# Sparse attention and a Fourier-mix block on one core: weight conversion on VectorE in a fixed plan, and two constant matmuls at each score step of the first attention

## The chip, the cores and the metric

The kernel runs on one core of one Trainium2 chip. The metric is the device time of one execution in microseconds. The engines are PE (TensorE, matmuls; PEld its weight loads), DVE (VectorE), ACT (ScalarE), POOL (GpSimd) and SP (SyncE, which issues nearly all DMAs). Each engine runs its own instructions in order.

## The reference

Four batches of 768 tokens; attention with 8 heads of 64, then a channel block of width 512 to 2048 and back. All in float32, but the two weights arrive as float64.

```python
k_sum = k.reshape(B, H, nb, block, D).max(axis=3)       # nb = 24 blocks of 32 tokens
v_sum = v.reshape(B, H, nb, block, D).mean(axis=3)
scores_l = scale * q @ k^T, kept where |i - j| < 16     # else -1e9
scores_s = scale * q @ k_sum^T + log(block)
a = softmax(concat(scores_l, scores_s)); x = a @ concat(v, v_sum)
mixed = real(fft(fft(x, axis=seq), axis=d_model))
u = x + mixed
un = (u - mean(u)) / sqrt(var(u) + 1e-6)
out = u + max(un @ w_ch1, 0) @ w_ch2
```

## The kernel before

**Attention** (`gen_attention`, L658). For each batch b and each of the four pairs of heads g, three steps with a yield after each. `scores` (L598): 96 small matmuls (L606) of a 64-token window of k against 32 tokens of q, exp on ACT (L610), a mask `near` multiplied in on DVE. `sum_scores` (L614) against the block maxima km, and `prepare` (L582) for the next pair: twelve 128x128 transposes (L590) of q and k, copied out by ACT in four copies (L591), and the block maxima by DVE (L592). `values` (L625): matmuls with the value windows vw (L638) and the block sums vs (L643), then reciprocal and product on DVE into x (L650). `load` (L534) fetches q and k of a pair, two DMAs of 256 B rows each; `load_values` (L559) the overlapping windows of v, also 256 B rows, and for every second pair `block_sums` (L543): two DMAs, then sums on POOL.

**Weights** (`convert` L678, `make_w1`, `make_w2`). The float64 weights are loaded as pairs of int32 in 32 pieces of 128x512 and turned into float32: two masks on DVE (L687, L688), two activations on ACT, two three-operand steps on DVE (L691, L693), and a product on POOL (L529, the helper `gtt`). Two pieces make a tile with four products of a Strassen-Winograd scheme, and four sums on POOL (`_left_sums`, `_right_sums`) make it seven. Eight w1 and eight w2 tiles are used for the first batch straight from SBUF (pools of three and four buffers) and written to DRAM (dw1, dw2), from where the later batches fetch them (`get_w1`, `get_w2`).

**Fourier step** (`gen_fourier`, L752). Sums and differences of x on DVE (tile `fold`), matmuls with tables (L786, output y), a second set (L806, L808, output mx) added to x, statistics, an inverse square root by four Newton steps on small tiles (`norm`), normalization (L833), transposes (L837, unt) and four sums into `u`.

**Channel step** (`gen_channel`, L844). Two halves (c) of four hidden tiles (j): for each j 28 matmuls (L863, outputs hx, hy, hz), combined and passed through a relu on DVE (L867) into `h`; then for each of three token pairs four sums of h on DVE (tile `s`), and matmuls with w2 (L906, outputs ox, oy, oz) added to x on DVE (helper `tt`, L526).

**Order.** The program text drives generators side by side (`drive`, L956): the first attention alone; the tables of the Fourier step; three weight tiles; then for each batch b four steps of its Fourier and channel generators to one step of the attention of batch b + 1, and for b = 0 one weight tile a round. The framework's planner then orders each engine's instructions by its own estimates, so two pieces of work without a dependency can change places. Pools of a fixed number of buffers make a load wait until an older tile is free, and SP issues in order.

Of the kernel before, what the change touches and what calls it, by code (L numbers as in the profile page):

```python
# [469 lines left out]
def _main_program(ctx, tc, q, k, v, moe_w_ch1, moe_w_ch2, out):  # L470
# [88 lines left out]
    def load_values(b, g):  # L559
# [3 lines left out]
        if g % 2 == 0:  # L563
            block_sums(b, g // 2)
# [17 lines left out]
    def prepare(b, g):  # L582
# [42 lines left out]
    def values(b, g, p, pm, x):  # L625
# [19 lines left out]
        for r in range(2):  # L645
            rc = rec[:, b * NP + g, r]
            nc.vector.reciprocal(out=rc, in_=av[r][:, :, D])
            for h in range(2):
                ts, c = slice(HT * h, HT * (h + 1)), P * g + D * (r ^ h)
                tt(x[:, ts, c:c + D], av[r][:, ts, 0:D], rc[:, ts, None].to_broadcast([P, HT, D]), ALU.mult)  # L650
# [7 lines left out]
    def gen_attention(b):  # L658
        x = bpool.tile([P, NST, DM], FP, tag="x", bufs=2, name=f"x_{b}")
        x_of[b] = x  # L660
        for g in range(NP):
            p = scores(b, g)
            yield
            pm = sum_scores(b, g)
            n1, n2 = following(b, g, 1), following(b, g, 2)
            if n1:
                prepare(*n1)
            yield
            values(b, g, p, pm, x)
            if n2:  # L670
                load(*n2)
                load_values(*n2)
# [3 lines left out]
    wt = {}  # L676

    def convert(name, dst, src, shape):  # L678


        n = shape[0] * shape[1]
        raw = bpool.tile([P, n, 2], I32, tag="raw", bufs=2, name=f"raw_{name}")
        nc.sync.dma_start(out=raw.rearrange("p (a n) w -> p a (n w)", a=shape[0]), in_=src)
        tmp = bpool.tile([P, 2, n], FP, tag="cvt", bufs=2, name=f"cvt_{name}")
# [5 lines left out]
        nc.scalar.activation(out=tmp[:, 1, :], in_=man, func=AF.Copy, bias=1.0, scale=2.0 ** -20)  # L690
# [334 lines left out]
```

## Time and profile before

| | us |
|---|---|
| median of 3 runs | 930.02 (928.06 to 930.32) |
| the profiled execution | 931.02 |
| its span in the trace | 929.2 |
| PE busy | 829.2 (89%) |
| DVE busy | 530.3 (57%) |
| ACT busy | 168.8 (18%) |
| POOL busy | 147.4 (16%) |

The span runs from the first to the last instruction of the trace. Matmuls are pipelined, so a busy PE need not be at its peak, and its clock is granted at one of two levels (1.2 and 2.4 GHz); the profile gives the mean of a stretch as a share of the higher. A wait costs something only on the engine that sets the end of its stage, so the views below are read by stage. In the timeline a number after the count in brackets is the idle time ahead of the instruction and what ended it.

### The profile page before, as it was taken

The page shows a single profiled execution, that of the slowest core. Times are in us where ns is not written, and L with a number is a line of the kernel's source. Part 1 is how long each engine was busy: PE and PEld are TensorE (multiplying, and loading weights), DVE is VectorE, ACT ScalarE, POOL GpSimd, SP SyncE. Part 2 cuts the span into 40 slices and gives each one's busy share as a digit, 9 for nine tenths or more (in the row PEclk, how much of TensorE's full clock was granted, in tenths as well). Part 3 has the DMA queues.
Part 4 walks back from the last instruction along what each step waited for, and adds up shares of the span by engine and source line. Part 5 has one row for each costly group of instructions (what it writes and reads, how often), then busy time and mean ns, then how long its engine had stood idle before and what let it go on. Part 6 is the DMA issues. An engine that isn't in the chain of part 4 may idle for free.

```text
span 929.2 us, 15289 instructions
## 1 busy us (share of the span) xinstructions
PE 829.2 (89%) x6386; PEld 618.3 (67%) x6386; DVE 530.3 (57%) x1158; ACT 168.8 (18%) x349; POOL 147.4 (16%) x142
## 2 busy tenths in 40 slices
PE   4778748687886799999999999999999997999997
PEld 3656634466753588657875888668857875587586
DVE  1366986799368964935423937635327556352252
ACT  2222312432023102221112012220021011200200
POOL 2230625567056700020000000000000000000000
PEclk9777859989898999999999999999999998999999
DMA  9995791777926508826162147321051161213101
GB/s 187 178 189 164 236 178 62 219 228 218 163 76 244 199 35 287 151 97 147 35 206 78 57 150 232 86 80 41 27 197 60 46 261 54 105 41 153 45 24 48
DMA packets 127917, 122.76 MB, mean 132 GB/s; under 512 B 102912, under 2 KB 111328, under 8 KB 127840
## 3 DMA queue, kind: packets, MB, share of 16 engines
q1 hardware_dynamic: 127296, 121.14, 46.9%
q8 instruction: 52, 0.85, 0.4%
q10 hardware_dynamic: 544, 0.56, 0.2%
q14 instruction: 25, 0.20, 0.1%
HBM read 100.71 MB, written 20.97 MB: 131 GB/s over the span
## 4 chain that ended last, share of the span: by engine, by line
PE 68%; DVE 20%; DMA 4%; POOL 3%; issue 3%; SPq 2%; ACT 1%; DVEq 0%; ACTq 0%; POOLq 0%
PE ox L906 17%; PE hx L863 15%; PE oz L906 8%; PE hz L863 7%; PE oy L906 4%; PE hy L863 4%; PE y L786 3%; DMA raw<-in_moe_w_ch_dram 2%; DVE cvt L688 2%; POOL w L529 2%; DVE cvt L693 2%; PE sc L606 2%; DVE cvt L691 2%; DVE x L526 2%; DVE cvt L687 2%
## 5 line engine op out<-in xcount | busy, mean ns | idle before, releaser
L863 PE MATMUL hx<-u,w 128*128 128x384 f32 x512 | 189.2, 500 | 15.5 <-ACT h L876 6.0
L863 PEld LDWEIGHTS hx<-u,w 128*128 128x128 f32 x512 | 97.9, 195 | 85.8 <-ACT h L876 8.9
L906 PE MATMUL ox<-w,h 128*128 128x256 f32 x384 | 93.9, 393 | 8.4 <-DVE x L526 7.9
L863 PE MATMUL hz<-u,w 128*128 128x384 f32 x256 | 96.6, 498 | 4.7 <-ACT h L878 4.7
L906 PE MATMUL ox<-w,s 128*128 128x256 f32 x384 | 92.8, 384 | 4.0 <-DVE x L526 3.5
L906 PE MATMUL oz<-w,s 128*128 128x256 f32 x384 | 93.0, 384 | 2.6 <-DVE s L526 2.6
L906 PEld LDWEIGHTS ox<-w,h 128*128 128x128 f32 x384 | 75.4, 197 | 22.8 <-DVE x L526 9.1
L906 PEld LDWEIGHTS ox<-w,s 128*128 128x128 f32 x384 | 72.0, 191 | 16.3 <-DVE x L526 5.6
L526 DVE TENSOR_TENSOR x<-ox,x 128x256 f32<-128x256 f32 x96 | 40.4, 422 | 74.2 <-PE ox L906 74.2
L906 PEld LDWEIGHTS oz<-w,s 128*128 128x128 f32 x384 | 73.3, 192 | 13.1 <-DVE s L526 2.9
L863 PEld LDWEIGHTS hz<-u,w 128*128 128x128 f32 x256 | 49.8, 195 | 40.3 <-POOL vb L529 5.3
L529 POOL TENSOR_TENSOR w<-cvt 128x512 f32<-128x512 f32 x32 | 43.6, 1364 | 133.2 <-DVE cvt L693 72.5
L529 POOL TENSOR_TENSOR w<-w 128x256 f32<-128x256 f32 x64 | 56.2, 893 | 3.1
L526 DVE TENSOR_TENSOR h<-hy,h 128x384 f32<-128x384 f32 x32 | 17.8, 555 | 67.5 <-PE hy L863 67.5
L526 DVE TENSOR_TENSOR h<-hx,h 128x384 f32<-128x384 f32 x32 | 17.8, 555 | 56.1 <-PE hx L863 56.0
L863 PE MATMUL hy<-u,w 128*128 128x384 f32 x128 | 46.5, 486 | 0.0
L906 PE MATMUL oy<-w,h 128*128 128x256 f32 x192 | 46.0, 380 | 0.3 <-POOL w L529 0.3
L606 PEld LDWEIGHTS sc<-qt,kt 64*64 64x64 f32 x1536 | 33.7, 157 | 12.7 <-issue 8.6
L606 PE MATMUL sc<-qt,kt 64*64 64x32 f32 x1536 | 36.7, 239 | 6.0 <-issue 3.7
L906 PEld LDWEIGHTS oy<-w,h 128*128 128x128 f32 x192 | 36.5, 191 | 5.8 <-POOL w L529 0.7
L867 DVE TENSOR_SCALAR h<-h 128x384 f32<-128x384 f32 x96 | 38.7, 404 | 2.9
L526 DVE TENSOR_TENSOR s<-h 128x512 f32<-128x512 f32 x48 | 39.2, 816 | 0.2
(92 smaller groups left out, 1043.3 us busy)
## 6 DMA issues: line engine op xcount, KB each, us to landing
w<-dw SPq DMA_DIRECT2D x48, 896.0 KB, 5.6
raw<-in_moe_w_ch_dram SPq DMA_DIRECT2D x32, 512.0 KB, 5.1
dw<-w SPq DMA_DIRECT2D x16, 896.0 KB, 4.3
vw<-in_v_dram SPq DMA_DIRECT2D x62, 192.0 KB, 5.7
kn<-in_k_dram SPq DMA_DIRECT2D x32, 192.0 KB, 5.3
qn<-in_q_dram SPq DMA_DIRECT2D x32, 192.0 KB, 5.2
vb<-in_v_dram SPq DMA_DIRECT2D x16, 384.0 KB, 6.3
out_dram<-x SPq DMA_DIRECT2D x24, 256.0 KB, 2.0
```

The lines of the kernel that those rows point to most:

```text
L526: nc.vector.tensor_tensor(out=out, in0=in0, in1=in1, op=op)
L529: nc.gpsimd.tensor_tensor(out=out, in0=in0, in1=in1, op=op)
L606: nc.tensor.matmul(ps[h][r:r + 64, i, :], kt[rows, o:o + 64], qt[rows, o:o + BLOCK], start=True, stop=True)
L687: nc.vector.tensor_scalar(out=ex, in0=high, scalar1=0x7FF00000, scalar2=None, op0=ALU.bitwise_and)
L688: nc.vector.tensor_scalar(out=man, in0=high, scalar1=0x000FFFFF, scalar2=None, op0=ALU.bitwise_and)
L691: nc.vector.scalar_tensor_tensor(out=ex, in0=high, scalar=-(1 << 31), in1=ex, op0=ALU.bitwise_and, op1=ALU.bitwise_or)
L693: nc.vector.scalar_tensor_tensor(out=tmp[:, 1, :], in0=low, scalar=2.0 ** -52, in1=tmp[:, 1, :], op0=ALU.mult, op1=ALU.add)
L786: nc.tensor.matmul(y, fgs[par][:, st, P * g:P * (g + 1)], fs[par][:, g % 2, st, :], start=(st == 0), stop=(st == HT - 1))
L863: nc.tensor.matmul(ps, w[:, a, kk, :], u[:, r, kk, :], start=start and kk == 0, stop=stop and kk == 1, skip_group_check=True)
L867: nc.vector.tensor_scalar(out=t, in0=t, scalar1=0.0, scalar2=None, op0=ALU.max)
L906: nc.tensor.matmul(ps, left[a][:, n, :], wt[2, b, j][:, r, :], start=start and n == 0, stop=stop and n == NC - 1, skip_group_check=True)
```

## The change

Weights: the product and the sums go from POOL to DVE (`gtt` to `tt`). A fixed plan says in which order the sixteen tiles are made, and from which stage of the first batch's channel step on; one generator makes them in small steps (three to a piece, two pieces, the sums, the store: eight to a tile). `load_raw` issues the raw loads up to three pieces ahead, from a pool of four buffers that the loads of `block_sums` now share. Four w2 tiles are staged: made in the `s` buffers, stored to DRAM and fetched again. The generator starts beside the first attention: 15 steps with five attention steps, 21 with the other seven, 20 in the first Fourier step, and the rest in the first channel step.

q and k: one DMA a tensor, with six consecutive tokens of a head in a partition (1536 B); each transpose then holds two token parities of one head, is written with a stride of three, and is copied out by ACT in halves of 64 partitions with a stride of two. `load` runs three pairs ahead instead of two.

`keep_busy`: two matmuls on `ident` and `near` after the scores and after the sum scores, for b == 0 only. In the first batch relu is on ACT; half of the normalization goes to ACT in every batch, and the Newton steps are three of three operations. `drive` spreads the steps evenly in a round.

```diff
     def load(b, g):
-        qn, kn = (apool.tile([P, NST, 2, D], FP, tag="nat", bufs=4, name=f"{n}n_{b}_{g}") for n in "qk")
+        qn, kn = (apool.tile([P, 2, NST * D], FP, tag="nat", bufs=4, name=f"{n}n_{b}_{g}") for n in "qk")
         for dst, src in ((kn, k), (qn, q)):
-            for e in range(2):
-                nc.sync.dma_start(out=dst[:, :, e, :], in_=src[b, 2 * g + e].rearrange("(t p) d -> p t d", p=P))
+            nc.sync.dma_start(out=dst, in_=src[b, 2 * g:2 * g + 2].rearrange("e (p t) d -> p e (t d)", p=P))
@@ block_sums
-        raw = [bpool.tile([4 * nb, hf, D], FP, tag="vb", bufs=2, name=f"vb_{b}_{gg}_{i}") for i in range(2)]
+        raw = [bpool.tile([4 * nb, hf, D], FP, tag="raw", bufs=4, name=f"vb_{b}_{gg}_{i}") for i in range(2)]
@@ load_values
-        if g % 2 == 0:
-            block_sums(b, g // 2)
+        if g % 2 and following(b, g, 1):
+            block_sums(*divmod((b * NP + g + 1) // 2, NP // 2))
@@ prepare
-            for h in range(2):
-                ps = abank([P, HT, P], f"qk_{b}_{g}_{h}")
+            for e in range(2):
+                ps = abank([P, S2], f"qk_{b}_{g}_{e}")
                 for i in range(HT):
-                    nc.tensor.transpose(ps[:, i, :], src[:, HT * h + i].rearrange("p e d -> p (e d)"), ident)
-                nc.scalar.copy(out=dst[:, S2 * h:S2 * (h + 1)], in_=ps.rearrange("p i c -> p (i c)"))
+                    nc.tensor.transpose(ps[:, i::HT], src[:, e, P * i:P * (i + 1)], ident)
+                for par in range(2):
+                    nc.scalar.copy(out=dst[D * e:D * (e + 1), par:S:2], in_=ps[D * par:D * (par + 1)])
@@ new
+    def keep_busy(b):
+        if b == 0:
+            ps = bank([P, 512], "idle")
+            for _ in range(2):
+                nc.tensor.matmul(ps, ident, near.rearrange("p h i c -> p (h i c)")[:, 0:512], start=True, stop=True)
@@ gen_attention
             p = scores(b, g)
+            keep_busy(b)
             yield
             pm = sum_scores(b, g)
...
+            if n3:
+                load(*n3)
+            keep_busy(b)
             yield
@@ convert, make
+    plan = [(1, 0, False, None), (1, 1, False, None), (2, 0, True, None), (1, 2, False, None), (2, 1, True, None),
+            (2, 2, True, None), (2, 3, True, None), (1, 3, False, ("h", 0, 0)), (1, 4, False, ("h", 0, 1)),
+            (1, 5, False, ("h", 0, 2)), (1, 6, False, ("h", 0, 3)), (2, 4, False, ("o", 0, 0)),
+            (1, 7, False, ("h", 0, 4))] + [(2, j, False, ("o", 0, 0)) for j in range(5, NJ)]
...
-        gtt(dst, vb, va, ALU.mult)
+        yield
+        tt(dst, tmp[:, 1, :], tmp[:, 0, :], ALU.mult)
+        yield
...
-        _left_sums(gtt, lambda i: w[:, i])
+        (_left_sums if f == 1 else _right_sums)(tt, part)
@@ gen_fourier
-            for _ in range(4):
-                tt(z, y, y, ALU.mult)
+            for _ in range(3):
+                nc.vector.scalar_tensor_tensor(out=z, in0=y, scalar=-0.5, in1=y, op0=ALU.mult, op1=ALU.mult)
                 tt(z, z, var, ALU.mult)
-                nc.vector.tensor_scalar(out=z, in0=z, scalar1=-0.5, scalar2=1.5, op0=ALU.mult, op1=ADD)
-                tt(y, y, z, ALU.mult)
+                nc.vector.scalar_tensor_tensor(out=y, in0=z, scalar=1.5, in1=y, op0=ADD, op1=ALU.mult)
...
+            if t % 2:
+                nc.scalar.activation(out=un[:, t, :], in_=x[:, t, :], func=AF.Identity, bias=shift[:, i:i + 1],
+                                     scale=y[:, i:i + 1])
@@ gen_channel
                 def relu(t):
-                    nc.vector.tensor_scalar(out=t, in0=t, scalar1=0.0, scalar2=None, op0=ALU.max)
+                    if b:
+                        nc.vector.tensor_scalar(out=t, in0=t, scalar1=0.0, scalar2=None, op0=ALU.max)
+                    else:
+                        nc.scalar.activation(out=t, in_=t, func=AF.Relu)
@@ main
+    block_sums(0, 0)
+    load_values(0, 0)
     load(0, 1)
-    load_values(0, 0)
     prepare(0, 0)
+    load_raw(1)
     load_values(0, 1)
+    load(0, 2)
...
-    drive((gen_attention(0), 1))
+    attn, weights = gen_attention(0), gen_weights()
+    drive((first(attn, 5), 1), (first(weights, 15), 3))
     get_tables(0)
-    drive((gen_weights(0, 3), 1))
+    drive((attn, 1), (first(weights, 21), 3))
     for b in range(B):
...
+        if b == 0:
+            drive((gen_fourier(0), 4), (first(weights, 20), 4), (first(attn, 5), 1))
+            drive((gen_channel(0), 4), (weights, 12), (attn, 1))
+        else:
+            drive((gen_post(b), 4), (attn, 1))
```

## Rows read from the trace of the kernel before

**Rows 1.** Engines' busy time by stage, from window to window.
```profile
core 0: us, PE busy (x) PEld busy (x) DVE busy (x) ACT busy (x) POOL busy (x), PEclk, DMA share, GB/s
0.00:58.20 58.20, 38.60 (x916) 31.44 (x916) 15.13 (x50) 15.39 (x33) 11.76 (x17) 0.85 1.04 185
58.20:80.40 22.20, 14.05 (x333) 10.34 (x331) 18.00 (x39) 4.15 (x9) 6.11 (x5) 0.60 1.09 243
80.40:137.20 56.80, 40.37 (x362) 33.99 (x359) 47.63 (x116) 17.35 (x34) 23.67 (x23) 0.71 0.72 176
137.20:350.60 213.40, 175.93 (x936) 122.94 (x935) 163.64 (x254) 50.54 (x92) 100.02 (x92) 0.92 0.55 158
350.60:549.00 198.40, 194.67 (x1571) 145.82 (x1570) 104.72 (x253) 31.55 (x71) 5.86 (x6) 1.00 0.45 127
```
**Rows 2.** DVE's groups, 80 to 351 us: count, busy us, mean ns, idle before.
```profile
L688 DVE TENSOR_SCALAR cvt<-raw 128x512 int32<-128x512 int32 x32 | 30.5, 952 | 0.0
L691 DVE SCALAR_TENSOR_TENSOR cvt<-raw,cvt 128x512 int32<-128x512 int32 x32 | 28.4, 889 | 0.6 <-ACT cvt L689 0.6
L693 DVE SCALAR_TENSOR_TENSOR cvt<-raw,cvt 128x512 f32<-128x512 uint32 x32 | 27.4, 855 | 0.0
L687 DVE TENSOR_SCALAR cvt<-raw 128x512 int32<-128x512 int32 x32 | 23.8, 744 | 13.9 <-DMA raw<-in_moe_w_ch_dram 10.6 <-POOL w L529 3.4
L526 DVE TENSOR_TENSOR s<-h 128x512 f32<-128x512 f32 x12 | 14.6, 1214 | 0.0
L867 DVE TENSOR_SCALAR h<-h 128x384 f32<-128x384 f32 x24 | 12.8, 539 | 0.5
```
**Rows 3.** DVE's groups from 400 to 590 us, one of them.
```profile
L526 DVE TENSOR_TENSOR s<-h 128x512 f32<-128x512 f32 x12 | 8.2, 684 | 0.1
```
**Rows 4.** POOL's groups over the whole span, the two of the weights.
```profile
L529 POOL TENSOR_TENSOR w<-w 128x256 f32<-128x256 f32 x64 | 56.2, 893 | 3.1
L529 POOL TENSOR_TENSOR w<-cvt 128x512 f32<-128x512 f32 x32 | 43.6, 1364 | 133.2 <-DVE cvt L693 72.5 <-PE hx L863 53.0 <-DVE norm L821 3.2
```
**Rows 5.** DVE's timeline: start us, us, instruction.
```profile
59.74 2.58 DVE L526 TENSOR_TENSOR fold<-x 128x1536 f32<-128x1536 f32 x1
...
85.84 0.42 DVE L687 TENSOR_SCALAR cvt<-raw 128x512 int32<-128x512 int32 x1
...
219.16 0.41 DVE L688 TENSOR_SCALAR cvt<-raw 128x512 int32<-128x512 int32 x1
219.49 0.68 DVE L526 TENSOR_TENSOR s<-h,s 128x512 f32<-128x512 f32 x1
220.09 0.68 DVE L691 SCALAR_TENSOR_TENSOR cvt<-raw,cvt 128x512 int32<-128x512 int32 x1
...
227.21 2.84 DVE L693 SCALAR_TENSOR_TENSOR cvt<-raw,cvt 128x512 f32<-128x512 uint32 x1
```
**Rows 6.** Waits over the whole span: us, times, longest.
```profile
PE vs L628 <- POOL vbs L529: 5.1, 1, 5.1
```
**Rows 7.** The DMA view, 0 to 62 us.
```profile
DMA packets 34554, 11.40 MB, mean 184 GB/s; under 512 B 33618, under 2 KB 33842, under 8 KB 34546
```
**Rows 8.** The window 350 to 360 us, columns as in the first group.
```profile
350.00:360.00 10.00, 10.00 (x120) 7.89 (x119) 3.24 (x8) 2.54 (x7) 0.00 (x0) 1.00 0.95 334
```
**Rows 9.** The chain that ended last, in order of time: start us, us, what.
```profile
249.49 1.73 PE oz L906 x8
...
256.81 1.29 PE hz L863 x4
...
325.71 3.50 PE ox L906 x8
...
361.38 1.46 PE qk L590 x12
...
389.45 1.29 PE hx L863 x4
```
**Rows 10.** ACT's groups, 350.6 to 549 us, the copies of the tables' output.
```profile
L792 ACT COPY big<-y 128x192 f32<-128x192 f32 x8 | 2.7, 334 | 44.7 <-PE y L786 44.7
```
**Rows 11.** PE's timeline in the last batch, the first transposes of `un`.
```profile
769.70 2.79 PE L837 MATMUL unt<-ident,big 128*128 128x128 f32 x12 [4.03 <-DVE norm L526]
```

More of the change, by code (lines that the diff above doesn't have):

```diff
@@ L709, in make_w2 @@
-    def make_w2(j):
-        w = bpool.tile([P, 7, HD], FP, tag="w2", bufs=NC, name=f"w2_0_{j}")
-        for hh in range(2):
-            r = P * (NJ * hh + j)
-            convert(f"2_{j}_{hh}", w[:, 2 * hh:2 * hh + 2], moe_w_ch2.bitcast(I32)[r:r + P, :].rearrange(
-                "p (a n) -> p a n", a=2), (2, HD))
-        _right_sums(gtt, lambda i: w[:, i])
-        nc.sync.dma_start(out=dw2[j], in_=w)
-        wt[2, 0, j] = w
+        yield
+        tt(dst, tmp[:, 1, :], tmp[:, 0, :], ALU.mult)
@@ new lines, in convert, with make @@
+        yield
+    def make(f, j, staged):
+        if staged:
+            t = [bpool.tile([P, n, HD], FP, tag="s", bufs=5, name=f"m{f}_{j}_{i}") for i, n in enumerate((2, 2, 2, 1))]
+            part = lambda i: t[i // 2][:, i % 2]
+            pair = lambda i: t[i]
+        else:
+            if f == 1:
+                w = bpool.tile([P, 7, 2, P], FP, tag="w1", bufs=3, name=f"w1_0_{j}")
+                wv = w.rearrange("p a k n -> p a (k n)")
+            else:
+                w = wv = bpool.tile([P, 7, HD], FP, tag="w2", bufs=NC, name=f"w2_0_{j}")
+            part = lambda i: wv[:, i]
+            pair = lambda i: wv[:, 2 * i:2 * i + 2]
+        for hh in range(2):
+            yield from convert((f, j, hh), pair(hh).rearrange("p a n -> p (a n)"))
+        (_left_sums if f == 1 else _right_sums)(tt, part)
+        yield
+        to = dw1[j].rearrange("p a k n -> p a (k n)") if f == 1 else dw2[j]
+        if staged:
+            for i, n in enumerate((2, 2, 2, 1)):
+                nc.sync.dma_start(out=to[:, 2 * i:2 * i + n], in_=t[i])
+            made.add((f, j))
+        else:
+            nc.sync.dma_start(out=to, in_=wv)
+            wt[f, 0, j] = w
+        yield
@@ L720, in get_w1, with gen_weights @@
+    def gen_weights():
+        for f, j, staged, stage in plan:
+            while stage and stage not in issued:
+                yield
+            yield from make(f, j, staged)
     def get_w1(b, j):
         w = bpool.tile([P, 7, 2, P], FP, tag="w1", bufs=3, name=f"w1_{b}_{j}")
+        if b == 0 and (1, j) not in made:
+            return
         nc.sync.dma_start(out=w, in_=dw1[j])
@@ L726, in get_w2 @@
         w = bpool.tile([P, 7, HD], FP, tag="w2", bufs=NC, name=f"w2_{b}_{j}")
+        if b == 0 and (2, j) not in made:
+            return
         nc.sync.dma_start(out=w, in_=dw2[j])
         wt[2, b, j] = w
-    def gen_weights(first, last):
-        steps = [(f, j) for c in range(0, NJ, NC) for f in (make_w1, make_w2) for j in range(c, c + NC)]
-        for f, j in steps[first:last]:
-            f(j)
-            yield
     tables = {}
@@ L792, in gen_fourier @@
                 nc.scalar.copy(out=ty[:, g, par:S2:2], in_=y[:, 0:F2])
-                nc.vector.tensor_copy(out=tr[:, g, par:S2:2], in_=ps[:, F2:0:-1])
+                nc.scalar.copy(out=tr[:, g, par:S2:2], in_=ps[:, F2:0:-1])
                 yield
@@ L872, in gen_channel @@
                 tt(c11, Y, c11, ADD)
-                relu(c11)
                 yield
@@ L878, in gen_channel @@
                 nc.scalar.copy(out=c22, in_=Z)
+                relu(c11)
                 yield
@@ L881, in gen_channel @@
                 tt(c22, X, c22, ADD)
-                relu(c22)
                 product(Z, S4, B22, False, True)
                 tt(c12, Z, c12, ADD)
-                relu(c12)
                 yield
@@ L888, in gen_channel @@
                 nc.scalar.activation(out=c21, in_=X, func=AF.Relu)
+                relu(c22)
+                relu(c12)
+                issued.add(("h", b, j))
                 yield
```

90 lines of the change are left out of this document (53 added, 37 removed).

## The prediction

> **What bounds the kernel now.** I read the stages first: what each engine does between the points where a Fourier step begins on TensorE [rows 1]. The Fourier and channel steps of the first batch, with the second attention beside them, take from 80.4 to 350.6, 270.2 us; those of the second batch take 198.4, with the same work except for the weight conversion. In that second stage PE is busy 194.67 us: it is bound by TensorE, and the change touches little of it. The reader is to see in [rows 1] that the first batch loses 71.8 us against its successor, that PE is idle there for 16.4 us of 56.8 and for 37.5 us of 213.4, and that it runs at a granted clock of 0.71 and 0.92 of full, so part of the time on the lower of its two levels. DVE is busy 47.63 + 163.64 = 211.3 us there, POOL 123.7.
>
> Then the groups of instructions on DVE in that stretch [rows 2], against the same operation once POOL has nothing left to do [rows 3], and POOL's own [rows 4]. A sum of two tiles of 128x512 (s<-h) takes 1214 ns instead of 684. The four DVE steps of a conversion take 952, 889, 855 and 744 ns on average, while the timeline has them at 0.41 and 0.68 us when POOL is still and once at 2.84 [rows 5]. So DVE waits for POOL, not for work.
>
> The Trainium skill, SBUF — State Buffer, section SBUF: two separate sides, has a reason: the two engines share one pair of ports, which one instruction holds to its end. It also holds the other way round, which speaks against loading DVE: the block sums of v stay on POOL, and by that sentence they would be late more often. The row that bears on it is PE vs, which waited 5.1 us once for POOL's vbs [rows 6]; twice that would make the sum 5 us worse, which is inside the range.
>
> Last the start. From 0 to 58.2 PE is busy 38.6 us and DVE 15.1, but the DMA engines are full: share 1.04 at 185 GB/s [rows 1], and 33618 of the 34554 packets up to 62 us are under 512 B [rows 7]. With large packets the same engines move 334 GB/s at a share of 0.95 [rows 8]. The first attention is bound by DMA. The conversion of weights begins only at 85.84 us, though the program emits three w1 tiles ahead of the Fourier step; the fold of that step, emitted after them, runs at 59.74 [rows 5]. The order on the engines is a planner's, not the text's.
>
> **The change, part by part.**
>
> *Products and sums move from POOL to DVE.* Removed from POOL: 43.6 + 56.2 = 99.8 us [rows 4]. Added to DVE: 32 products of 128x512 and 64 sums of 128x256. A two-input operation of 512 columns is followed by the next after 0.60 us (220.09 less 219.49), a mask after 0.33 (219.49 less 219.16) [rows 5]; a sum of 256 columns I take at 0.33, half of 0.60 and a little. So a piece costs 2 x 0.33 + 3 x 0.60 = 2.46 us, a weight tile (two pieces, four sums) 6.2, sixteen of them 100 us of DVE. Before, the four DVE steps alone took 30.5 + 28.4 + 27.4 + 23.8 = 110.1 us [rows 2]. DVE pays nothing for the added work if the waiting for POOL goes. The bounds: nothing regained, then 32 x 0.60 + 64 x 0.33 = 40 us more on DVE, or all of it, then 10 less. I take the second, since the rows at rest repeat.
>
> *DVE in the first batch after.* From 211.3: the sums of s, 14.6 us for 12 [rows 2], fall to 8.2 (-6.4); the relu, 12.8 us there, goes to ACT (-12.8); conversions -10; and 4.5 of the 16 weight tiles (36 steps of 8 to a tile are driven beside the first attention) move to a stage where DVE is busy 15 of 58 us, -28. That leaves 154 against 194 of PE in a stage that lasts 198 if nothing waits. PE becomes the bound of this stage too.
>
> *Where it will still wait.* Five tiles (w2 4 to 7, w1 7) can be emitted only after the first half of the channel step's output, and are wanted by the end of the next four hidden steps: 5 x 6.2 us and some 6 of the steps' own make 37 us of DVE beside 36 of PE (28 matmuls in each step, four in 1.29 us [rows 9]). That is even, so a few us of wait. The Fourier step lasts 38.8 us in the second batch (350.6 to the first hx at 389.45 [rows 9]) and 56.8 in the first; with 2.5 tiles of conversion beside it, 16 us of DVE, I take the middle. I put the whole stage at 198.4 + 20, bounds +5 and +45 (the latter keeps two thirds of today's 71.8).
>
> *The first attention.* q and k now come as one DMA each, 1536 B to a packet. For a pair of heads these are 0.79 MB: at 178 GB/s (185 / 1.04) 4.4 us, at 350 GB/s (334 / 0.95) 2.2 [rows 1, 8]; four pairs save 0 to 9 us. But into the same queue come 12 raw pieces of 0.52 MB, the stores of four tiles of 0.92 MB and the tables of 1.9 MB, 12 MB in all, 34 us at 350 GB/s. They were there before too, but after 66 us. What the last values step needs stands behind about half of that, so +17 - 9 = +8 us: the attention ends near 66 instead of 58. The tables are then there in time, the first fold takes 9 us (59.74 on, before), and PE's first y is at 76. Bounds 66 (the traffic hidden) and 92 (all of it ahead). SP issues these loads one after another, and a raw load waits for its buffer (four, now shared with the block sums of v); behind it on SP stand q, k and the value windows, and PE waits for those.
>
> *The two matmuls on constants.* 16 of 128x512 in all, only for b == 0. Eight of 256 columns take 1.73 us at the high level and 3.50 at the low one [rows 9], so one of 512 takes 0.43 to 0.88, together 7 to 14 us of PE. They lie in PE's waits for exp and for DMA; without that cover they cost up to 14. What they could bring: the granted clock is 0.60 between 58.2 and 80.4 [rows 1], where PE is busy 14.05 us.
>
> The Trainium skill, TensorE: Matmul & The Clock Gate, section What's actually happening, says that the clock falls when PE rests and returns with activity. By that sentence the first y would begin up to 5 us earlier. I take 0 for both: DMA ends last in this stage.
>
> *q and k in the later stages.* As many transposes as before, 0.12 us each (12 in 1.46 [rows 9]), now written with a stride of three into PSUM. No row shows that form: I take 0, and the upper end is rival 4. ACT makes eight copies of 64 partitions instead of four of 128, 384 columns each; at 334 ns for 192 columns written with a stride of two [rows 10] a copy takes at most 0.67 us, so at most 2.7 us more for each pair of heads, below the channel step's work between a pair's transposes and its scores. ACT is busy 31.55 of 198.4 us [rows 1].
>
> *Small chains.* Newton steps 4 to 3 with three operations each, half of the normalization on ACT, w1 fetched ahead. PE waited 4.03 us for that chain in the last batch, where no attention covers it [rows 11]. I take -1.3 us for each of three batches, -4, bounds 0 and -10.
>
> **The sum.** First y at 76; first batch 218.4; from 350.6 to the end at 929.2 it is 578.6 us today, less 4. 76 + 218.4 + 574.6 = 869.0 us of span. The profiled execution took 931.02 for a span of 929.2, so 1.8 lie around it: 870.8. The median of the runs, 930.02, is 1.0 below that execution, so 870.
>
> **The rivals.**
> 1. *Early weight traffic bounds the first attention.* For it: a share of 1.04 today [rows 1], and 12 MB more. First y at 92, the rest as forecast: 887; with the first batch at 225 too, 893.
> 2. *DVE, in order, still bounds the first batch.* Each conversion step stands in DVE's queue ahead of the relu, sums and masks that PE waits for. Loss 45 instead of 20: 896. Against it: 154 us of work in 218.
> 3. *The early start doesn't happen*: the planner again puts conversions behind the fold, as it did with three tiles [rows 5]. First y at 68, but 28 us more of DVE beside PE, first batch 235: 879.
> 4. *Slower: the strided transposes.* All stages after the first batch are PE's. If a transpose with its columns three apart costs four times as much, 0.48 instead of 0.12, its 192 cost 69 us: 940. It decides from 0.12 + 60 / 192 = 0.43 us each. For it: no row shows that form. Against it: ACT's copies at a stride show no such price.
> 5. *No change*: rivals 1, 2 and 4 in part, together the 60 us.
>
> **How the numbers follow.** Forecast (850 to 885) 0.55, rival 1 0.15, rival 2 0.12, rival 3 0.08, rival 4 0.06, rival 5 0.04. About 0.3% is what a measurement of this kernel can tell from no change: faster by more 0.90, within it 0.04, slower 0.06. Low end: y at 66, a first batch of 205, and -6 in the small chains: 66 + 205 + 572.6 + 1.8 = 845. High end 906: rivals 1 and 2 with half of each other's loss. Left out are rivals 4 and 5 and some 0.08 at the ends.
>
> **What would show it.** Right: no w on POOL; conversion steps at 0.42 and 0.68 us throughout, products at 0.68, sums near 0.41; conversions from about 15 us on; first y near 76, second near 294, the next stage 198 as before; a granted clock near 1 in the first channel step. Wrong: first y after 90 with the DMA share at 1 (rival 1); PE waiting for DVE's cvt or w in the channel step (rival 2); conversions behind the fold (rival 3); transposes over 0.2 us each and later stages over 200 (rival 4).

## The result, and the profile after

The changed kernel takes 901.57 us (median of 4 runs, 900.2 to 910.82) against 929.04 (927.87 to 930.32): ratio 0.9725, interval 0.9658 to 0.9792. It is faster by 27.5 us where 60 were forecast. Its profiled execution took 901.99 us, with a span of 900.2.

Engines' busy time by stage in the changed kernel, from window to window; the stages end where [rows 1] end, at the first `y` and the first `hx` of a batch, and the last line is the third batch's Fourier step:

```profile
core 0: us, PE busy (x) PEld busy (x) DVE busy (x) ACT busy (x) POOL busy (x), PEclk, DMA share, GB/s
0.00:96.54 96.54, 68.06 (x1067) 47.34 (x1067) 54.88 (x117) 42.98 (x82) 17.61 (x21) 0.76 1.00 245
96.54:151.37 54.83, 47.69 (x569) 37.46 (x569) 46.26 (x114) 20.78 (x46) 6.37 (x5) 0.78 0.66 167
151.37:321.50 170.13, 160.50 (x912) 114.74 (x912) 132.29 (x260) 57.43 (x111) 22.70 (x18) 0.99 0.62 184
321.50:521.33 199.83, 196.56 (x1598) 146.39 (x1596) 96.71 (x222) 45.04 (x98) 0.63 (x2) 1.00 0.41 124
521.33:562.08 40.75, 37.50 (x576) 29.88 (x574) 20.38 (x62) 18.89 (x44) 0.00 (x0) 1.00 0.66 214
```

| stretch, us | before | forecast | after |
|---|---|---|---|
| start to first `y` | 80.4 | 76 | 96.5 |
| first to second `y` | 270.2 | 218.4 | 225.0 |
| second to third `y` | 198.4 | 197.1 | 199.8 |
| third to fourth `y` | 195.6 | 194.3 | 198.7 |
| fourth `y` to the end | 184.6 | 183.3 | 180.1 |

The first batch gave up 45.2 us, near the 51.8 forecast; the first channel step fell from 213.4 to 170.1 at a granted clock of 0.99. Against that the first `y` came 16.1 us later instead of 4.4 earlier, and the two middle batches became 4.5 us longer instead of 2.6 shorter. The forecast for the profiled execution was 870.8 us, 31.2 less than it took: 20.5 of these lie ahead of the first `y`, 6.6 in the first batch, 7.1 in the middle batches, and the last batch gives 3.2 back.

DVE's groups from the first to the second `y` (columns as in [rows 2]); they answer to [rows 2, 3]:

```profile
L728 DVE SCALAR_TENSOR_TENSOR cvt<-raw,cvt 128x512 int32<-128x512 int32 x23 | 18.4, 799 | 3.3 <-ACT cvt L725 3.3
L526 DVE TENSOR_TENSOR w<-w 128x256 f32<-128x256 f32 x36 | 18.2, 533 | 0.2
L730 DVE SCALAR_TENSOR_TENSOR cvt<-raw,cvt 128x512 f32<-128x512 uint32 x23 | 17.4, 755 | 0.7 <-ACT cvt L726 0.7
L526 DVE TENSOR_TENSOR w<-cvt 128x512 f32<-128x512 f32 x18 | 16.7, 936 | 1.4 <-PE hx L914 1.4
L724 DVE TENSOR_SCALAR cvt<-raw 128x512 int32<-128x512 int32 x23 | 9.7, 422 | 0.0
...
L526 DVE TENSOR_TENSOR s<-h 128x512 f32<-128x512 f32 x12 | 8.5, 706 | 0.6 <-ACT h L921 0.6
```

The masks are down from 952 to 422 ns and the sum of `s` from 1214 to 706. POOL's `w` groups of [rows 4] are gone, but POOL still makes its block sums of v (29 us in this stretch), and beside them the two-input steps stay above their 0.68. The block sums ahead of the first `y`, and a step beside them:

```profile
73.91 2.67 POOL L529 TENSOR_TENSOR vb<-vb,vb 96x1024 f32<-96x1024 f32 x1 [41.72 <-DMA vb<-in_v_dram]
```
```profile
74.83 2.30 DVE L728 SCALAR_TENSOR_TENSOR cvt<-raw,cvt 128x512 int32<-128x512 int32 x1 [0.45 <-ACT cvt L725]
```

The last part of the first `y`'s delay is seen in some 10 us. The timelines of DVE, ACT and PE ahead of it (start, us, instruction, idle before and its releaser):

```profile
85.20 1.75 DVE L526 TENSOR_TENSOR fold<-x 128x1536 f32<-128x1536 f32 x1
...
89.42 0.42 DVE L724 TENSOR_SCALAR cvt<-raw 128x512 int32<-128x512 int32 x1
89.75 0.95 DVE L526 TENSOR_TENSOR fold<-fold 128x768 f32<-128x768 f32 x1
93.50 0.69 DVE L728 SCALAR_TENSOR_TENSOR cvt<-raw,cvt 128x512 int32<-128x512 int32 x1 [2.80 <-ACT cvt L725]
94.11 0.69 DVE L730 SCALAR_TENSOR_TENSOR cvt<-raw,cvt 128x512 f32<-128x512 uint32 x1
...
95.85 0.55 DVE L526 TENSOR_TENSOR fold<-fold 128x381 f32<-128x381 f32 x1
```
```profile
88.59 2.10 ACT L593 COPY kt<-qk 64x384 f32<-64x384 f32 x4 [0.30 <-PE qk L591]
90.72 2.01 ACT L593 COPY qt<-qk 64x384 f32<-64x384 f32 x4
92.75 0.72 ACT L725 ACTIVATE cvt<-cvt,rebias 128x512 int32<-128x512 int32 x1
```
```profile
90.22 0.53 PE L630 MATMUL vs<-vbs,sel 96*128 96x64 f32 x2
96.54 1.98 PE L834 MATMUL y<-fs,fold 128*128 128x193 f32 x5 [5.79 <-DVE fold L819]
```

The rest of the fold stands in DVE's order behind a conversion step (L728). That step waits for ACT's L725, which stands in ACT's order behind the eight copies of q and k of 64 partitions, 4.1 us in a row. PE waits 5.79 us for what is left of the fold. The fold itself starts at 85.20 instead of 59.74 [rows 5], so most of the delay lies ahead of these timelines; from the start of the fold to the first `y` it is 11.3 us, against 20.7 before.

### The profile page after: what moved, and what is told of

The parts are those of the page before. It is cut to its first block, busy times and chain, and to the rows that moved or that the text cites. A ratio compares the mean times of both kernels' runs of the same rounds, so it can differ in the third digit from the quotient of the medians.

```text
span 900.2 us, 15323 instructions
## 1 busy us (share of the span) xinstructions
PE 837.3 (93%) x6418; PEld 617.4 (69%) x6418; DVE 500.6 (56%) x1106; ACT 231.2 (26%) x481; POOL 47.3 (5%) x46
## 2 busy tenths in 40 slices
DMA packets 88749, 126.43 MB, mean 140 GB/s; under 512 B 53504, under 2 KB 70624, under 8 KB 88672
## 5 line engine op out<-in xcount | busy, mean ns | idle before, releaser
L914 PE MATMUL hx<-u,w 128*128 128x384 f32 x512 | 186.7, 495 | 8.9 <-DVE h L526 6.0
L914 PEld LDWEIGHTS hx<-u,w 128*128 128x128 f32 x512 | 96.0, 192 | 77.3 <-DVE h L526 9.9
L914 PE MATMUL hz<-u,w 128*128 128x384 f32 x256 | 93.9, 486 | 0.0
L961 PE MATMUL ox<-w,h 128*128 128x256 f32 x384 | 89.6, 380 | 0.1
L961 PEld LDWEIGHTS ox<-w,h 128*128 128x128 f32 x384 | 72.6, 190 | 11.7 <-DMA w<-dw 0.4
L840 ACT COPY big<-y 128x192 f32<-128x192 f32 x32 | 10.7, 335 | 138.5 <-PE y L834 138.4
L834 PE MATMUL y<-fs,fold 128*128 128x193 f32 x192 | 37.2, 342 | 7.2 <-DVE fold L819 5.8
L924 ACT COPY h<-hx 128x384 f32<-128x384 f32 x32 | 15.3, 479 | 101.1 <-PE hx L914 94.8
L594 DVE TENSOR_REDUCE km<-kt 128x24 f32<-128x768 f32 x16 | 15.2, 949 | 46.8 <-ACT kt L593 46.8
L834 PEld LDWEIGHTS y<-fs,fold 128*128 128x128 f32 x192 | 32.3, 195 | 10.8 <-DVE fold L819 6.0
L725 ACT ACTIVATE cvt<-cvt,rebias 128x512 int32<-128x512 int32 x32 | 23.1, 721 | 62.7 <-DVE cvt L723 62.6
```

Source lines behind the costliest of these rows:

```text
L594: nc.vector.tensor_reduce(out=km[:, 0:nb], in_=kt[:, W:W + S].rearrange("p (n f) -> p n f", f=BLOCK), op=ALU.max, axis=AX.X)
L725: nc.scalar.activation(out=ex, in_=ex, func=AF.Relu, bias=rebias, scale=8.0)
L834: nc.tensor.matmul(y, fgs[par][:, st, P * g:P * (g + 1)], fs[par][:, g % 2, st, :], start=(st == 0), stop=(st == HT - 1))
L840: nc.scalar.copy(out=ty[:, g, par:S2:2], in_=y[:, 0:F2])
L914: nc.tensor.matmul(ps, w[:, a, kk, :], u[:, r, kk, :], start=start and kk == 0, stop=stop and kk == 1, skip_group_check=True)
L924: nc.scalar.copy(out=c11, in_=X)
```

## The experiments

In these, L numbers are each kernel's own.

**One part alone, or taken back.** e4 is the kernel before with nothing but the move from POOL to DVE; e3 is the changed kernel with that move undone (`gtt` for `tt` in `convert` and `make`). The edit of e4:

```diff
-        gtt(dst, vb, va, ALU.mult)
+        tt(dst, vb, va, ALU.mult)
-        _left_sums(gtt, lambda i: w[:, i])
+        _left_sums(tt, lambda i: w[:, i])
-        _right_sums(gtt, lambda i: w[:, i])
+        _right_sums(tt, lambda i: w[:, i])
```

> The kernel before with nothing changed but product and sums of the weights on DVE instead of POOL. If the port is the loss: DVE's conversion steps at 0.42 and 0.68 us, first batch 235 to 250 us instead of 270, whole 895 to 910. If the order is what counts: first batch 262 to 275, whole within 0.8% of 930.

> The changed kernel with product and sums of the weights back on POOL, in the new plan. If the waiting between DVE and POOL was the loss: conversion steps again at 0.7 to 1.0 us on average, first batch (first y to second y) 240 to 255 us instead of 225, whole 915 to 930. If the early start and the order are what gains, and POOL's help is worth as much as it costs: first batch 220 to 230, whole 895 to 907.

e4 took 897.15 us (896.48 to 898.35), ratio 0.9641 (0.9614 to 0.9668): the move alone gains 33 us, more than the whole change. e3 took 914.14 (913.46 to 916.12). DVE's groups in the first batch, of e4 and then of e3:

```profile
L526 DVE TENSOR_TENSOR w<-w 128x256 f32<-128x256 f32 x64 | 25.5, 429 | 0.0
L526 DVE TENSOR_TENSOR w<-cvt 128x512 f32<-128x512 f32 x32 | 24.3, 763 | 0.7 <-PE hx L863 0.7
L691 DVE SCALAR_TENSOR_TENSOR cvt<-raw,cvt 128x512 int32<-128x512 int32 x32 | 22.1, 692 | 2.7 <-ACT cvt L689 2.7
...
L688 DVE TENSOR_SCALAR cvt<-raw 128x512 int32<-128x512 int32 x32 | 13.9, 436 | 0.0
```
```profile
L728 DVE SCALAR_TENSOR_TENSOR cvt<-raw,cvt 128x512 int32<-128x512 int32 x23 | 22.5, 978 | 5.7 <-ACT cvt L725 5.7
...
L724 DVE TENSOR_SCALAR cvt<-raw 128x512 int32<-128x512 int32 x23 | 15.5, 674 | 0.0
```

In e4 the mask is at 436 and L691 at 692, against 952 and 889 in [rows 2]: with POOL's weight work gone DVE does all of it at nearly the price of rest. In e3, with that work on POOL again, they are at 674 and 978, and the first batch takes 237.7 us instead of 225.0. e4 doesn't separate DVE's slower steps beside POOL from its waits for POOL's results and for raw pieces (3.4 and 10.6 us in [rows 2]); the move takes away the first two and leaves 2.6 us of the third. So everything else in the change together costs some 4 us (901.6 against 897.2); the rest of the runs ask which parts. The plan, relu on ACT and the small chains were not taken back one by one.

**The layout of q and k.** e7 is the changed kernel with `load` and `prepare` of before. e9 keeps the new loads and the strided transposes, and takes one ACT copy of a whole bank for the two half copies (tokens of q and k then stand in another order):

```diff
-                for par in range(2):
-                    nc.scalar.copy(out=dst[D * e:D * (e + 1), par:S:2], in_=ps[D * par:D * (par + 1)])
+                nc.scalar.copy(out=dst[:, S2 * e:S2 * (e + 1)], in_=ps)
```

> The changed kernel with q and k loaded, transposed and copied as in the kernel before (256 B rows, four ACT copies of 128 partitions a pair instead of eight of 64). If the new layout costs the later stages (second to third y 199.8 and third to fourth 198.7 us, against 194.3 and 195.6 with the old layout in the run with nothing changed but the weights on DVE): these return to 195 to 196 and the whole gains 5 to 8 us less what the slower loads cost the start (0 to 9). If the layout is free there: both stay within 1 us, and the first y is 3 us or more later.

> The changed kernel, with one ACT copy of 128 partitions x 384 for each PSUM bank of transposed q or k in place of two copies of 64 partitions x 384; loads, transposes and their strided PSUM writes stay. So the tokens of q and k stand in another order and the attention computes something else: this run is read for its time alone. With the layout of before (e7) the stretch from the third to the fourth first y fell from 198.7 to 195.4 us, and its Fourier step from 40.75 to 37.1. If the doubled number of ACT copies (8 of 0.50 us a pair in place of 4 of 0.49) is the cause, by standing in ACT's order between the Fourier step's own copies and TensorE: that stretch falls to about 195.5, the Fourier step to about 37, the second y to about 317, and the whole to 885-890. If it is the strided transposes or the loads: the stretch stays at 198.7 and the whole at about 901.

e7 took 886.80 us (886.58 to 892.31), ratio 0.9546 (0.9506 to 0.9585), the fastest of the runs that compute the whole; it beats both kernels. The gain of 14.8 us is more than the 5 to 8 expected, and the first `y` comes 3.4 us earlier, not later. e9 took 887.01 (884.72 to 890.4). The stages of e9, as in the first fence of this part:

```profile
0.00:90.51 90.51, 64.06 (x1066) 45.78 (x1066) 56.48 (x117) 29.85 (x58) 17.70 (x21) 0.77 1.03 251
90.51:141.12 50.61, 43.16 (x568) 33.92 (x569) 45.92 (x114) 18.31 (x42) 6.37 (x5) 0.87 0.76 200
141.12:312.80 171.68, 161.27 (x913) 115.41 (x912) 133.87 (x260) 52.87 (x104) 24.10 (x18) 0.98 0.62 181
312.80:509.30 196.50, 195.93 (x1598) 146.63 (x1597) 96.81 (x222) 35.44 (x82) 0.63 (x2) 1.00 0.42 126
509.30:546.38 37.08, 36.51 (x530) 29.48 (x529) 20.27 (x62) 14.11 (x36) 0.00 (x0) 1.00 0.72 234
```

Against the changed kernel the first `y` is 6.0 us earlier, the first batch 2.7 shorter, the middle batches 3.3 each and the last 1.0 longer; the third Fourier step takes 37.08 instead of 40.75. There the changed kernel's ACT groups and PE's waits were these:

```profile
L593 ACT COPY qt<-qk 64x384 f32<-64x384 f32 x8 | 4.0, 504 | 0.1
L593 ACT COPY kt<-qk 64x384 f32<-64x384 f32 x8 | 4.0, 502 | 0.1
```
```profile
PE unt L891 <- ACT big L884: 1.4, 1, 1.4
PE mx L854 <- ACT big L840: 0.7, 1, 0.7
```

and e9's copies there:

```profile
L592 ACT COPY qt<-qk 128x384 f32<-128x384 f32 x4 | 1.9, 498 | 0.0
...
L592 ACT COPY kt<-qk 128x384 f32<-128x384 f32 x4 | 1.7, 484 | 0.0
```

A copy of 64 partitions takes 504 ns, one of 128 takes 498. Twice as many copies are twice the time, and in the Fourier step they stand in ACT's order ahead of its writes to `big` on which PE waits (L840 copies the tables' output, L884 is ACT's half of the normalization). In e9 both waits for `big` are gone; they are 2.1 of the 3.7 us by which its step is shorter. The strided transposes and the dense loads are in e9 too, so neither costs anything that can be seen. Nor do the dense loads gain anything over the whole: e7 moves its data in 130221 packets, e9 in 88749, and they take the same time. Up to the first `y` e9 is 2.6 us ahead (90.5 against 93.1), which is the most that they can be worth there.

**The early start.** e2 is the changed kernel with all 56 early weight steps beside the first Fourier step; e14 the same with the old layout; e8 is e14 without the matmuls on constants.

```diff
-    drive((first(attn, 5), 1), (first(weights, 15), 3))
+    drive((first(attn, 5), 1))
-    drive((attn, 1), (first(weights, 21), 3))
+    drive((attn, 1))
-            drive((gen_fourier(0), 4), (first(weights, 20), 4), (first(attn, 5), 1))
+            drive((gen_fourier(0), 4), (first(weights, 56), 12), (first(attn, 5), 1))
```

> The changed kernel with all 56 early weight steps beside the first Fourier step and none beside the first attention. If the early weight work (its DMA traffic and its waits on SP and DVE) delays the first attention: first y at 68 to 78 us instead of 96.5; the Fourier step then takes the conversions, 70 us or more instead of 54.9, so the whole stays between 890 and 910. If the weight work is not the cause: first y stays over 90 and the whole goes to 915 or more.

> The changed kernel without the early start, without the fill and with the old q and k; what is left is DVE alone, the plan from the first Fourier step on, relu on ACT and the small chains. If these three are each a loss or nothing, as the first runs suggest for two of them: first y at 74 to 80, second y at 305 to 316, the rest 572 to 576, whole 882 to 893. If the three belong together with the rest: 897 or more.

> e7 with all early weight steps beside the first Fourier step and none beside the first attention. With the new layout this moved nothing (e2: 903.1 against 901.6). If the early start is worth nothing with either layout: 885-889, the first y at 75-80 and the second at 317. If the early start pays once ACT's copies are halved, because ACT's time was what the early pieces had to share: 895-904, with the second y at 325-333, as in e8, which had in addition no matmuls on constants and took 904.

e2 took 903.08 us (900.02 to 907.79), e14 904.01 (901.55 to 906.97), e8 904.01 (901.27 to 905.44). The first `y` is at 80.0, 77.3 and 73.9. So the early start is worth 17.2 us with the old layout (904.0 to 886.8) and 1.5, within the spread, with the new one (903.1 to 901.6); and the new layout costs 14.8 us with the early start and nothing without it.

The difference does not lie in the first attention: there the early start costs 15.8 us with the old layout (first `y` at 93.1 against 77.3) and 16.6 with the new one (96.5 against 80.0). It lies in what the early start gives back in the first Fourier step, which then has fewer conversions beside it. This step in e7, e2 and e14 (54.83 us in the changed kernel, 50.61 in e9):

```profile
93.10:132.60 39.50, 36.78 (x508) 30.49 (x509) 37.80 (x100) 15.61 (x37) 6.15 (x5) 0.91 0.82 193
```
```profile
80.00:153.90 73.90, 41.55 (x553) 33.87 (x554) 65.05 (x166) 31.75 (x64) 0.00 (x0) 0.77 0.61 189
```
```profile
77.31:152.44 75.13, 44.95 (x548) 35.24 (x549) 64.06 (x154) 25.58 (x54) 8.77 (x5) 0.75 0.69 183
```

The early start shortens it by 35.6 us with the old layout (e14 to e7) and by 19.0 with the new (e2 to the changed kernel). Why by less with the new one was not taken apart: 4.2 us are ACT's copies (e9), and a part is order, since the changed kernel runs 569 matmuls in this step and e7 508.

e14's middle batches are 7.6 and 3.3 us shorter than e2's (192.3 and 195.4 against 199.9 and 198.8), and its second `y` is 13.3 later. A part of that is order too: e14's stretch from the second to the third `y` holds 118 matmuls less, the scores, sum scores and transposes of one pair of heads, and PE is busy 191.7 us there against 196.6. The rest stays open. So does a loss that e8 shows: against e4 it has the plan from the Fourier step on, the new order of the loads, relu on ACT and the small chains, and its first batch takes 259.0 us against 243.0.

**What holds the first attention.** Each of these takes one demand of the early pieces away, and with it part of the computation: e5 loads only the first two raw pieces and converts them over and over (these two and the block sums' loads have buffers of their own), e11 leaves out ACT's two steps for the first nine pieces, e12 DVE's five. The edits of e5, e11 and e12, in this order:

```diff
+            if len(raws) >= 2:
+                raws.append(raws[len(raws) % 2])
+                continue
...
-        nc.scalar.activation(out=ex, in_=ex, func=AF.Relu, bias=rebias, scale=8.0)
-        nc.scalar.activation(out=tmp[:, 1, :], in_=man, func=AF.Copy, bias=1.0, scale=2.0 ** -20)
+        if i >= 9:
+            nc.scalar.activation(out=ex, in_=ex, func=AF.Relu, bias=rebias, scale=8.0)
+            nc.scalar.activation(out=tmp[:, 1, :], in_=man, func=AF.Copy, bias=1.0, scale=2.0 ** -20)
...
+        if i < 9:
+            nc.scalar.activation(out=ex, in_=high, func=AF.Relu, bias=rebias, scale=8.0)
+            nc.scalar.activation(out=dst, in_=high, func=AF.Copy, bias=1.0, scale=2.0 ** -20)
...
+            return
```

> The changed kernel with only the first two of the 32 raw pieces loaded; the other conversions read these two again, so the output is not the reference's. DVE, ACT and PE have the same work; 15.7 MB of DMA and SP's waits for a raw buffer are gone. If the weights' DMA traffic and its queueing bound the first attention: first y at 80 to 86 us instead of 96.5, second y 12 us or more earlier than 321.5. If DVE's order or the fill is the bound: first y 92 or later, second y at 316 or later.

> The changed kernel without ACT's two instructions in the first nine weight pieces, those beside the first attention (the output is not the reference's for that reason). The first y was at 96.5 with the pieces and at 80.0 without any of them (e2). If the pieces delay the attention through ACT (DVE waits 9.3 us for ACT's conversions before that first y, and the attention's own copies and exponentials stand behind ACT's conversions): first y at 82-88. If DVE's order is the cause (54.8 us of DVE work before that first y in place of 31.4 in e2): first y at 92-96. If neither, but transfers: 94 or later.

> The changed kernel without DVE's five instructions on each of the first nine weight pieces; ACT's two instructions read the raw piece and write the tile, and the sums, loads and stores stay (the output is not the reference's for that reason). If DVE's order delays the first attention: first y at 80-86, near e2's 80.0. If ACT's order does: first y at 92-96. If both take part: 86-92 in this run and in the one without ACT's instructions. If transfers do: 94 or later in both.

The first `y` was at 94.3 in e5, 92.8 in e11 and 87.5 in e12 (96.5 in the changed kernel), the whole at 899.35, 899.20 and 882.25, one execution each. The stretch up to the first `y` in e12 and in e14:

```profile
0.00:87.54 87.54, 63.89 (x1066) 45.98 (x1067) 27.90 (x72) 40.19 (x76) 16.13 (x21) 0.77 1.01 243
```
```profile
0.00:77.31 77.31, 58.27 (x1090) 41.03 (x1091) 27.95 (x62) 19.69 (x42) 16.88 (x21) 0.85 1.15 205
```

With nearly all raw traffic gone the first `y` comes 2.2 us earlier, with ACT's conversions gone 3.7, with DVE's steps gone 9.0, with the half copies gone (e9) 6.0, and with all early pieces gone (e2) 16.6. Each of these is read from one traced execution. e12's span is 19.7 us shorter (900.2 and 880.5): 9.0 of these lie at the first `y`, 5.5 in the first batch and 5.2 in the next. The gains at the first `y` lie in two places. The fold starts at 85.20 in the changed kernel, 87.17 in e5, 85.23 in e11, 81.62 in e12, 81.71 in e9 and 69.62 in e2; from there to the first `y` it is 11.3, 7.1, 7.6, 5.9, 8.8 and 10.4 us. So the whole gain of e11 and 5.4 us of e12's lie among the steps of the fold, where the timelines above show a conversion step in its order. Ahead of the fold no single demand explains more than 3.6 us of the 15.6 that e2 gains there. Two more things take part. PE itself is slower up to the first `y`: 1067 matmuls in 68.06 us at a granted clock of 0.76 in the changed kernel, against this line of e2:

```profile
0.00:80.00 80.00, 60.79 (x1091) 42.10 (x1091) 31.43 (x62) 33.41 (x66) 24.06 (x26) 0.83 1.09 226
```

And where one demand is gone, another wait ends last. In e12 PE waits 12.8 us for v's windows ahead of its first `y` (1.3 in the changed kernel), and SP, in order, waits 11.8 us for DVE's sums ahead of a store:

```profile
PE av L640 <- DMA vw<-in_v_dram: 12.8, 3, 7.9
```
```profile
SPq L768 <- DVE w L526: 11.8, 1, 11.8
```

e5, e11 and e12 all keep the stores of weight tiles in SP's order, so these runs don't say what that order costs. DMA's share is 0.97 to 1.15 in every one of these kernels, with the first `y` anywhere from 77 to 97: a full share by itself does not tell that DMA ended last.

**The two matmuls on constants.** e1 is the changed kernel without the two matmuls, e13 is e7 without them.

```diff
             p = scores(b, g)
-            keep_busy(b)
             yield
...
-            keep_busy(b)
             yield
```

> The changed kernel without the two constant matmuls at each score step. Theory A (they hold PE back: in the trace of the changed kernel 22 of their 32 records run in one block from 16.2 to 27.4 us, ahead of the second pair's transposes): the first y moves from 96.5 to 85 to 90 us and the whole to 890 to 895. Theory B (DMA traffic or SP's order bounds the first attention, the block only fills a wait): first y within 2 us of 96.5, whole 899 to 904. Theory C (they keep the granted clock up and help): first y later, whole 905 or more.

> e7 (the changed kernel with the q and k layout of before, 886.8) without the two matmuls on constants. With the new layout they cost 3 us (e1). If what they do is the same here: 884, first y at 90, second at 315. If they hold TensorE's granted clock up or fill its waits where the transposes come sooner, so that their removal costs: 895 or more, and the granted clock of the first 80 us lower than in e7. That run without them and with the other DMA queue (e10) took 899.1 would then be due to the matmuls; otherwise to the queue.

e1 took 898.41 us (895.49 to 903.3), e13 890.32 (885.93 to 891.63). Without them one kernel is 3.2 us faster and the other 3.5 slower, and both ranges overlap with those of the kernel that has them: no effect that can be told. In e1 the first `y` comes 4.5 us earlier (92.1) and the first batch takes 2.6 longer, which is neither of the first two cases expected. PE's timeline of the changed kernel shows that they don't stand where the text puts them:

```profile
16.17 11.23 PE L660 MATMUL idle<-near,ident 128*128 128x512 f32 x22
27.23 0.82 PE L591 MATMUL qk<-ident,kn 128*128 128x128 f32 x6
27.89 1.02 PE L660 MATMUL idle<-near,ident 128*128 128x512 f32 x2
```

Of their 32 records 22 run in one block of 11 us, ahead of the second pair's transposes. In e1 those transposes start at 18.68 instead of 27.23, and the second `y` comes 1.9 us earlier.

**The queue.** e6 is the changed kernel with the raw loads and the stores of weight tiles issued on POOL's queue, e15 is e7 with that, e10 is e15 without the matmuls on constants.

```diff
-            nc.sync.dma_start(out=raw.rearrange("p (a n) w -> p a (n w)", a=a), in_=src)
+            nc.gpsimd.dma_start(out=raw.rearrange("p (a n) w -> p a (n w)", a=a), in_=src)
...
-            nc.sync.dma_start(out=to, in_=wv)
+            nc.gpsimd.dma_start(out=to, in_=wv)
```

> The changed kernel with the raw loads and the stores of the weight tiles issued from POOL instead of SP: the same bytes, but SP no longer waits for DVE (10.1 us before the first store, 6.8 before a load) with q, k and v behind it. If SP's order is the cause of the late first y: 84 to 90 us instead of 96.5 and the whole 889 to 896. If the traffic itself is the bound: first y 94 or later, whole 898 to 906.

> e7 with raw weight loads and weight-tile stores issued on POOL's queue. With the new layout that gave 8 us (e6). If the queue is worth the same here: 879, second y at 310. If it hurts once q and k come in 256-byte pieces from both heads (130 thousand packets in place of 89 thousand): 895-900 as e10, with PE waiting more for kn, qn and vw before the first y (e10: 24.0 us for kn and qn, 12.2 for vw; e7: none and 8.7).

> The changed kernel with the q and k layout of before (as e7, 886.8), without the two matmuls on constants (as e1, 3 us less than the changed kernel) and with the raw weight loads and weight-tile stores on POOL's DMA queue (as e6, 8 us less). If the three gains add: about 876. If the gains of e6 and e7 are the same one (both bring the second y to 316-317): about 884. If the queue on POOL gets in the way of other loads once the q and k loads issue more transfers: above 890.

e6 took 893.56 us (888.98 to 897.06), 8 less than the changed kernel, and that in neither of the ways expected: its first `y` did not move (97.0), and the gain lies in the first batch (218.7 against 225.0). e15 898.56 (896.08 to 901.35), 12 more than e7; e10 899.14 (896.35 to 899.75). In e10 PE waited before its first `y` (at 103.1) for q, k and v:

```profile
PE qk L591 <- DMA kn<-in_k_dram: 15.5, 3, 8.6
PE ss L621 <- DVE x L526: 13.1, 2, 9.5
PE av L639 <- DMA vw<-in_v_dram: 12.2, 2, 10.5
```

In e15, with its first `y` at 104.3, those waits are short (1.9 us for q and k, 4.9 for v). What all three have more of is PE waiting for DVE's product x: 6.2 us in e6, 13.1 in e10, 9.0 in e15, and 0.9 in e7. So the queue's loss with the old layout is shown, and its gain with the new one; the cause of neither is. The Trainium skill (SBUF — State Buffer, SBUF: two separate sides) names a candidate: GpSimd writes the descriptors of the transfers that it issues, and can't while DVE runs a step in a two-port mode. No run here shows which of DVE's steps run so, or tells this cause from others.

## Why the prediction was wrong where it was

**Right: what bounded the first batch.** DVE waited for POOL, and it takes over the 100 us of products and sums for nothing: e4 gains 33 us by that alone, and DVE's busy time in its first batch is 199.4 us against 211.3. First to second `y` took 225.0 us against 218.4 forecast. The sum of DVE's work came out at 178.6 us (46.3 + 132.3) instead of 154; the steps beside POOL's block sums cost some 12 us of it (the six groups of the fence and L723, 9.7 us more, are 98.6 us; with the two-input steps at 0.68 and 0.42 they would be 86.2). That is read from the trace; no run takes the block sums away, and the other 12 us were not traced. The sentence drawn from the Trainium skill (SBUF — State Buffer, section SBUF: two separate sides), that an instruction holds the shared ports to its end, agrees with the trace where DVE is the one that is late: L728 took 2.30 us at 74.83, while POOL summed v. The other way round, the late `vbs` that I priced by it at 5 us did not come: PE's `vs` never waited for it.

**Wrong: the first attention, "+17 - 9 = +8 us".** This term is the largest miss: the first `y` at 96.5 instead of 76, 20.5 of the 31.2 us between forecast and profiled execution. I read a DMA share of 1.04 as the bound, and priced early weights as bytes. The -9 for denser loads is at most 2.6 at the first `y` and nothing in the whole (e7, e9). Of the +17 for bytes, the raw pieces, some 5 of the 12 MB, are worth 2 (e5). What the step left out is the order on the engines. The early pieces delay the first `y` by some 16 us with either layout: without them it is at 80.0 (e2), 77.3 (e14) and 73.9 (e8), near the 76 of the forecast. Conversion steps stand among the attention's and the fold's steps on DVE (9.0 us, e12) and on ACT (3.7, e11), and the copies of q and k, doubled, stand among both (6.0, e9). How these, SP's order and the lower clock make up the 15.6 us ahead of the fold stays open. I counted ACT's copies for the later stages only, and DVE's 28 us as free because DVE was busy 15 of 58. A free engine in order is not free when the waits of one chain hold up the other, as L728 does above.

**Wrong: "below the channel step's work".** At most 2.7 us of copies a pair, costed at nothing. It measured 2.2 (4.0 + 4.0 for two pairs against 1.9 + 1.7), so the size was right; but they don't lie in the channel step. They lie in the Fourier step, where PE waits for ACT's writes to `big`, and cost 3.3 us in each of two batches. Over the whole, the copies make 14.4 of the 31.2 us (spans 900.2 and 885.8), of which the 6.0 at the first `y` are also in the term above.

**Right in part.** The small chains show in the last batch, where no attention covers them. The wait of [rows 11] fell from 4.03 to 2.82, and PE's wait for the normalized x from 2.7 to 2.2, together 1.7 us against the 1.3 forecast there. The batch itself took 180.1 us against 184.6, but other runs with the same small chains take up to 183.7 (e11), and e4 without them 183.8, so the 4.5 is not theirs for sure. In the middle batches, where I had put two thirds, they give nothing that can be seen (195.4 in e9 against 195.6). The matmuls on constants were taken at 0, and 0 is what can be told, though they take 17.0 us of PE and not the 7 to 14 of the sum. The Trainium skill (TensorE: Matmul & The Clock Gate, What's actually happening) says that activity releases the throttle of the clock; from that I had drawn a first `y` up to 5 us earlier. In e7, with them, it is at 93.1, in e13, without them, at 93.7, and the granted clock up to there is 0.74 and 0.72; in the changed kernel and e1 it is 0.76 and 0.73, and the first `y` comes later with them. So these runs show no gain that follows from the sentence.

**The rivals.** Rival 1 came nearest in the first `y` (92), rival 2 in the whole (896). Rival 1's mechanism falls for the raw traffic: without it the first `y` moves by 2.2 us. Rival 2 is half true: DVE's order holds up PE, but mostly in the first attention and its fold; in the first channel step PE waits 6.0 us for DVE's `h`. Rival 3 falls: conversion begins at 30.75 us, ahead of the fold, though later than the 15 forecast. Rival 4 falls: e9 keeps the strided transposes and loses nothing. Rival 5 falls: 27.5 us is far outside the spread. Missing was a rival in which the early start and the new layout depend on each other: the early start is worth 17.2 us with the old layout and 1.5 with the new. That is shown, and the traces, one of each kernel, put the difference in the first Fourier step; its cause is shown for 4.2 us only, ACT's copies. With the old layout the change is at 886.8, 2 us above the 850 to 885 of the forecast.

## What to carry to other kernels

Before work is put beside a stage because an engine is idle there, write down that engine's order in the stage and ask, for each added step, what it may wait for and which step of the stage's own chain stands behind it. An ACT copy of half the partitions takes as long as a whole one, so a layout that halves the DMA packets and doubles the copies is paid on ACT. A change of several parts should be run with each part taken back: here three edited lines (e4) gave more than the whole.

## What the runs showed of the hardware

An ACT copy from PSUM of 64 partitions x 384, written at a stride of two, takes 504 ns, as long as one of 128 x 384 (498). A transpose of 128 x 128 written at a stride of three into PSUM costs no more than a dense one: 282 ns in the record, and 195.4 us from the third to the fourth `y` with either (e9 and e7). q and k in packets of 1536 B instead of 256 B changed nothing in the whole (886.8 and 887.0 us), though the DMA engines' share was at 1.03 to 1.08 up to the first `y` in both. A DVE step of 512 columns with two inputs (L728) took 2.30 us at 74.83 and 2.63 at 104.48, both times beside POOL's sums of v, and 0.69 alone.
